# An adaLN block with linear attention: the state products taken head by head, in blocks of 32 columns

## The chip, the cores and the metric

The kernel runs on one core of one Trainium2 chip. Its metric is the device time of one execution in microseconds (us). A core has TensorE (PE in the profile; PEld is its weight load), VectorE (DVE), ScalarE (ACT), GpSimd (POOL) and SyncE (SP), each with a program of its own, and DMA queues that several of them issue to.

## The reference

x has 2048 rows of 640, in 32 heads of 20 columns.

```python
mod = (silu(c) @ w_mod).reshape(1, 6, 1, -1)          # sa, ca, ga, sb, cb, gb
h = layernorm(x) * (1 + ca) + sa
q, k, v = split_heads(h @ wqkv)                        # 32 heads of 20
phi_q = concat(softmax(q @ w_phi), softmax(-q @ w_phi))    # 40 features a head
phi_k = concat(softmax(k @ w_phi), softmax(-k @ w_phi))
kv  = einsum("bhsf,bhsd->bhfd", phi_k, v)              # the state, 40 x 20 a head
z   = einsum("bhsf->bhf", phi_k)
num = einsum("bhqf,bhfd->bhqd", phi_q, kv)
den = einsum("bhqf,bhf->bhq", phi_q, z) + 1e-6
x = x + ga * ((num / den) @ wo)
h = layernorm(x) * (1 + cb) + sb
x = x + gb * (relu(h @ w1 + b1) ** 2 @ w2 + b2)        # 1728 wide
```

## The kernel before

The 2048 rows are 16 row tiles of 128, worked in pairs (t and t + 1 for even t). The projections k, v and q (`proj`, its products on the line of `mm`, L80) are sums of three products of a high and a low part. Each tile's 640 columns are made in two halves, 384 and 256 (`CUT`); TensorE's pieces of it are pk, pv and pq.

For each tile, k and q become features: `spread` subtracts the maximum and the minimum of each head (eq and ek, 128 x 1280: for each sign 640 columns), `exps` takes exponentials on ScalarE, and for k `k_norm` (L448 to L450) divides on VectorE by the sums, the last step being one product of 1280 columns. ek of tile t is `EK[t]`.

*State products.* `v_out` (L426 to L429) copies v from PSUM to the tile `vt[t % 2]` on ScalarE, four copies a tile. `vt` has 11 units of 64 columns: the 20 columns of three heads, a column of ones, three of zeros (the last unit has two heads). `do_kv` then makes one float32 product for each unit (L457): its 64 columns of `vt` are the stationary side, the same three heads' 2 x 60 features in ek the moving one. The product also holds what one head's v makes with another head's features, which is not used; the column of ones makes z. Units with even numbers use the left 64 columns of TensorE, the odd ones the right 64, and the sums over all 16 tiles stay in two PSUM banks (kvp). `do_kv` runs for two tiles at once, eight times in all, behind the v projection of the next pair's first tile and ahead of its q projection. Each float32 product shows as two loads and two products in the profile.

*The switch.* After the last pair, three ScalarE copies bring the state to SBUF (kvs, L797 to L799). `make_z`, inside the q projection of tile 13, spreads the row of each z over 128 rows by products with a broadcast column of the identity, four products in two row tiles of TensorE (64 rows each, L823), and copies them to zb (L831 to L835). `kv_diags`, in the q projection of tile 14, turns kvs by five transposes of 128 columns (L844) and a small one (L845), and does a few turns for the modulation vectors (mc, L308). `kv_out` copies the turned tiles (kvt) to kvd on ScalarE, and `kv_mask5` and `kv_masks` multiply them on VectorE by masks that leave each head its own block.

*Numerators.* `e_prod` multiplies the features of q with zb (L884) and adds them up, `e_recip` inverts, `e_tail` (L909) and `e_main` scale the features; ut holds the last two heads' ones. TensorE turns them (`tail_turn` L936, `tr_e` L954), multiplies them with kvd (`tail_num`, `num`), and goes on with wo.

*What sets the order.* In the start, and again from the last pair's k projection on, every engine runs in the order in which the code is written. In tiles 2 to 13 TensorE runs in written order; the other engines' order comes from a scheduler that sets it by its own costs of the instructions. DMA goes over queues issued from SP, ACT and POOL.

Of the kernel before, what the change touches and what calls it, by code (L numbers as in the profile page):

```python
# [20 lines left out]
F = 1728  # L21
NT = S // P
# [31 lines left out]
def kernel(  # L54
# [37 lines left out]
    def heads(ap):  # L92
        return ap.rearrange("p (h d) -> p h d", d=DH)
# [25 lines left out]
    def row(tag, name):  # L119
        return (pc if tag in ("s3", "s4") else mem).tile([P, D], F32, tag=tag, name=name, bufs=BUFS[tag])  # L120
# [19 lines left out]
    def tp(name):  # L140
        return psA.tile([P, 512], F32, tag="tp", name=name)
# [38 lines left out]
    mask5 = pc.tile([80, 40], F32, name="mask5")  # L180
    pc.tile([P, 24], F32, name="gap3")
    for v in vt:
        nc.gpsimd.memset(v, 0.0)
        nc.gpsimd.memset(v[:, :, 60:61], 1.0)

    def head_mask(m, rows, n, at):

        m3 = m.rearrange("p (h d) -> p h d", d=DH)
        nc.gpsimd.affine_select(out=m3, in_=m3, compare_op=ALU.is_ge, fill=0.0, base=-at,
                                pattern=[[-DH, n], [0, DH]], channel_multiplier=1)  # L190
        nc.gpsimd.affine_select(out=m3, in_=m3, compare_op=ALU.is_ge, fill=0.0, base=DH - 1 + at,
                                pattern=[[DH, n], [0, DH]], channel_multiplier=-1)

    mtmp = row("s2", "mtmp")[:120, :60]
    nc.gpsimd.memset(mask, 0.0)
    nc.gpsimd.memset(mask[:, :60], 1.0)
    nc.gpsimd.memset(mtmp, 1.0)
    head_mask(mask[:, :60], 120, 3, 0)
    head_mask(mtmp, 120, 3, 60)
    nc.gpsimd.tensor_tensor(mask[:, :60], mask[:, :60], mtmp, op=ALU.add)  # L200
    nc.gpsimd.memset(mask5, 1.0)
    nc.gpsimd.memset(mtmp[:80, :40], 1.0)
    head_mask(mask5, 80, 2, 0)
    head_mask(mtmp[:80, :40], 80, 2, 40)
    nc.gpsimd.tensor_tensor(mask5, mask5, mtmp[:80, :40], op=ALU.add)


    nc.scalar.dma_start(bdc[:120, :120], bd)
    nc.scalar.dma_start(c_t, c)
# [92 lines left out]
    def mod_turn(part, p, *cs_):  # L302
        t = MT.setdefault(part, None) or row("s1", f"mt{part}")
        MT[part] = t
        a, n = cs_[0] * P, len(cs_) * P
        for i, c in enumerate(cs_):
            src = by_turn(MA[part])[:, c] if part in (3, 4) else MA[part][:, c * P : (c + 1) * P]
            nc.tensor.transpose(p[:, i * P : (i + 1) * P], src, ident)  # L308
        nc.scalar.activation(t[:, a : a + n], p[:, :n], AF.Copy)
# [79 lines left out]
    def t1(j, *ds, more=None):  # L389
        if 0 in ds:  # L390
            HT[j] = ht(f"hT{j}", j)
        p = tp(f"ta{j}_{ds[0]}")
        for k, d in enumerate(ds):
            t_in(XB[j], d, p[:, 256 * k : 256 * k + 256])
        if more:
            mod_turn(more[0], p[:, 256:], 4)
        for k, d in enumerate(ds):
            t_out(cols_a, HT[j], d, f"a{j}", p[:, 256 * k : 256 * k + 256])
        DONE[:] = newest(ET_.Activation), newest(ET_.DVE)
        if more:  # L400
            mod_sum(*more)

    def proj(nm, t, *between):
        p = pj(f"p{nm}{t}")
        j, i = divmod(t, 2)
        s = slice(i * P, (i + 1) * P)
        for h, (a, b) in enumerate(CUT):
# [12 lines left out]

    def do_v(t):
        v_out(t, proj("v", t))
# [28 lines left out]

    def do_kv(t):
        v, e = vt[t % 2], EK[t]
        for u, (o, n) in enumerate(UN):
            g, c = divmod(u, 2)
            a = 120 * (g % 4)
            nc.tensor.matmul(  # L457
                kvp[g // 4][64 * c : 64 * c + 64, a : a + 2 * n].rearrange("p (s n) -> p s n", s=2),
                v[:, u], e[:, :, o : o + n],
                start=(t == 0 and g % 4 == 0), stop=(t == NT - 1), skip_group_check=True,  # L460
            )

    def do_q(t, *between):
# [249 lines left out]
    for t in range(2, NT - 2):  # L713
# [13 lines left out]
        p = proj("v", t, *([(1, 0, lambda: t1(j + 1, 4))] if t == NT - 3 else []))  # L727
        if i == 0:
            do_kv(t - 2)
            do_kv(t - 1)  # L730
# [73 lines left out]
    def bank(nm):  # L804
        return psB.tile([P, 512], F32, tag="m", name=nm)
# [6 lines left out]
    nc.gpsimd.memset(kv_t[96:, :640], 0.0)  # L812
    nc.gpsimd.tensor_copy(
        kv_t[96:, :640].rearrange("p (b n) -> p b n", n=64)[:, :, 60:],
        ident[96:, None, 120:124].to_broadcast([32, 10, 4]),
    )
    def make_z():
        at = [(c, b) for b in range(2) for c in range(2)]
        ps = {}
        for c, b in at:  # L820
            r, a, n = slice(64 * c, 64 * c + 64), 480 * b, ((480, 200), (480, 120))[c][b]
            p = ps[c, b] = tp("z") if len(ps) == 3 else bank(f"z{c}_{b}")
            nc.tensor.matmul(p[:, :n], ident[r, 64 * c + 60 : 64 * c + 61].to_broadcast([64, P]),  # L823
                             kvs[r, a : a + n], start=True, stop=True)
        for c, b in at:
            g0, m, p = 4 * b, (4, 1)[b], ps[c, b]
            for h in range(2):
                dst = zb[:, h, 120 * g0 : 120 * (g0 + m)].rearrange("p (g c n) -> p g c n", c=2, n=60)[:, :, c]
                src = p[:, : 120 * m].rearrange("p (g s n) -> p g s n", s=2, n=60)[:, :, h]
                if h:  # L830
                    nc.vector.tensor_copy(dst, src)  # L831
                else:
                    nc.scalar.activation(dst, src, AF.Copy)
            if (c, b) == (0, 1):
                nc.vector.tensor_copy(zb[:, :, 600:640], p[:, 120:200].rearrange("p (s n) -> p s n", s=2))  # L835

    q_out(q0 + 1, proj("q", q0 + 1, (0, 9, make_z)))

    kvt = [None, None]

    def kv_diags():
        kvt[:] = [bank(f"kvt{b}") for b in range(2)]
        for g in range(5):
            nc.tensor.transpose(kvt[g // 4][:120, (g % 4) * P : (g % 4) * P + P], kvs[:, 120 * g : 120 * g + 120], ident)  # L844
        nc.tensor.transpose(kvt[1][:80, P : P + 40], kvs[:40, 600:680], ident[:40, :40])  # L845
        mod_turn(5, kvt[1][:, 2 * P :], 4)
        mod_turn(5, bank("mc5"), 0, 1, 2, 3)

    def kv_out():
        nc.scalar.activation(kv5, kvt[1][:80, P : P + 40], AF.Copy)  # L850
        for b, (g0, g1) in enumerate(((0, 4), (4, 5))):
            nc.scalar.activation(kv_t[:120, P * g0 : P * g1], kvt[b][:120, : (g1 - g0) * P], AF.Copy)

    def kv_mask5():
        nc.vector.tensor_tensor(kv5, kv5, mask5, op=ALU.mult)

    def kv_masks():
        k = kv_t[:120, : 5 * P].rearrange("p (g n) -> p g n", n=64)
        nc.vector.tensor_tensor(k, k, mask[:, None, :].to_broadcast([120, 10, 64]), op=ALU.mult)


    ET, EU, EPT, OT = {}, {}, {}, {}
# [332 lines left out]
    e_recip(1)  # L1195
    load_e(3)
    do_q(q0 + 2, (1, 0, kv_diags))
    kv_out()
    e_tail(1)
    kv_mask5()  # L1200
    e_main(1)
# [599 lines left out]
```

## Time and profile before

| | |
|---|---|
| three runs | 751.80, 751.52, 750.88 us; median 751.52 |
| the profiled execution | 751.83 us, of which the span is 750.1 |
| TensorE's granted clock | 1.000 |
| busy: TensorE, VectorE, ScalarE, GpSimd | 744.9, 601.4, 457.5, 169.0 us |
| share of the span | 99%, 80%, 61%, 23% |

The span runs from the first to the last instruction that the profile records; the execution's time has a little around it. A row of the groups reads: line, engine, operation, output <- input by the program's names, TensorE's tile (rows*columns), shape and type, count | busy us, mean ns of one | idle us ahead of them. A row of the chain reads: start, length, engine, what, line, and how many instructions in a row. A row of the windows reads: window and its length, then for PE, PEld, DVE, ACT, POOL the busy us and the count, and behind them TensorE's clock, the DMA share and GB/s. Busy times of TensorE's products overlap where blocks of it run side by side, so the mean of one is then no cost of one.

### The profile page before, as it was taken

To read this page: it belongs to the slowest core of one execution; us is meant where nothing else is said; L and a number is where in the kernel's file an instruction comes from. 1 tells how busy PE (TensorE), PEld (TensorE's weight loads), DVE (VectorE), ACT (ScalarE), POOL (GpSimd) and SP (SyncE) were. 2 spreads that over 40 slices of the span, in tenths; PEclk is the share of its full clock that TensorE was granted. 3 is DMA by queue.
4 is the path that set the end of the run, shared out by engine and by line. 5 is a ranking of instruction groups with operands and counts; after the bars stand their busy time and mean duration, and the time that the engine had idled before them with its cause. 6 is when DMAs were issued, how large, how long until landed. Compare 5 with 4: busy or idle time off the path is not lost.

```text
span 750.1 us, 15320 instructions
## 1 busy us (share of the span) xinstructions
PE 744.9 (99%) x5854; PEld 728.3 (97%) x5854; DVE 601.4 (80%) x1089; ACT 457.5 (61%) x1065; POOL 169.0 (23%) x355
## 2 busy tenths in 40 slices
PE   9999999999999999999999999999999999999998
PEld 9999999999999998998999999999999999999997
DVE  6598987988998899999665778777777776777766
ACT  5767666667863355557587766475574756647431
POOL 3000101000100237647303040132221313223110
PEclk9999999999999999999999999999999999999999
DMA  9811432343432254663885576797667767667461
GB/s 330 335 36 77 155 93 81 107 140 107 137 101 81 57 189 160 150 148 109 195 236 183 158 212 227 252 343 204 180 198 200 222 183 227 191 172 218 127 184 36
DMA packets 58796, 126.39 MB, mean 168 GB/s; under 512 B 7438, under 2 KB 16403, under 8 KB 58723
## 3 DMA queue, kind: packets, MB, share of 16 engines
q1 hardware_dynamic: 38636, 79.20, 32.2%
q0 software_dynamic: 17504, 40.90, 21.8%
q10 hardware_dynamic: 2583, 5.30, 1.9%
q8 instruction: 46, 0.75, 0.4%
q14 instruction: 27, 0.22, 0.1%
HBM read 100.74 MB, written 29.89 MB: 174 GB/s over the span
## 4 chain that ended last, share of the span: by engine, by line
PE 98%; ACT 1%; DVE 1%; POOL 0%; issue 0%; ACTq 0%; POOLq 0%
PE up L80 25%; PE acc L80 18%; PE pq L80 9%; PE pk L80 9%; PE pv L80 9%; PE pwo L80 9%; PE acc3x L80 5%; PE kvp L457 3%; PE te L954 2%; PE numa L80 1%; PE foldk L282 1%; PE numb L80 1%; PE ta L364 1%; PE foldq L282 1%; PE warm L625 1%; PE mrow L586 1%
## 5 line engine op out<-in xcount | busy, mean ns | idle before, releaser
L80 PE MATMUL up<-h,w 128*128 128x256 f32 x1640 | 204.6, 276 | 0.1
L80 PEld LDWEIGHTS up<-h,w 128*128 128x128 f32 x1640 | 196.5, 188 | 0.7 <-DVE h L90 0.5
L1350 ACT ACTIVATE ft<-up,b_t 128x256 f32<-128x256 f32 x104 | 49.0, 471 | 96.0 <-PE up L80 95.6
L80 PE MATMUL acc<-w,ra 128*128 128x384 f32 x452 | 97.5, 335 | 0.0
L80 PE MATMUL pwo<-wo,ot 128*128 128x384 f32 (+1 forms) x480 | 78.4, 314 | 0.0
L1351 DVE TENSOR_TENSOR ft<-ft 128x256 f32<-128x256 f32 x104 | 43.8, 421 | 43.1 <-ACT ft L1350 41.4
L80 PE MATMUL pq<-wq,hT 128*128 128x384 f32 (+1 forms) x480 | 75.6, 312 | 0.0
L80 PEld LDWEIGHTS acc<-w,ra 128*128 128x128 f32 x452 | 72.7, 188 | 0.8 <-DVE ra L90 0.6
L80 PE MATMUL pk<-wk,hT 128*128 128x384 f32 (+1 forms) x480 | 72.7, 308 | 0.0
L80 PEld LDWEIGHTS pwo<-wo,ot 128*128 128x128 f32 x480 | 69.7, 188 | 2.8 <-issue 2.7
L80 PEld LDWEIGHTS pq<-wq,hT 128*128 128x128 f32 x480 | 71.1, 188 | 0.6 <-issue 0.2
L80 PE MATMUL pv<-wv,hT 128*128 128x384 f32 (+1 forms) x480 | 71.6, 306 | 0.0
L80 PEld LDWEIGHTS pk<-wk,hT 128*128 128x128 f32 x480 | 70.5, 188 | 0.4 <-issue 0.2
L80 PEld LDWEIGHTS pv<-wv,hT 128*128 128x128 f32 x480 | 70.0, 188 | 0.0
L90 DVE TENSOR_TENSOR ra<-ft,ra 128x384 fp32r<-128x384 f32 (+2 forms) x86 | 36.8, 449 | 32.6 <-ACT ra L1374 20.0
L1460 POOL DMA_DIRECT2D ring_a<-td_a x34 | 18.5, 543 | 116.9 <-PE acc L80 103.6
L1374 ACT ACTIVATE ra<-ft 128x384 fp32r<-128x384 f32 x48 | 25.2, 526 | 28.4 <-DVE ft L1351 22.4
L80 PE MATMUL acc3x<-w,ra 128*128 128x256 f32 x231 | 39.5, 278 | 0.0
L80 PEld LDWEIGHTS acc3x<-w,ra 128*128 128x128 f32 x231 | 37.2, 188 | 0.0
L1365 DVE TENSOR_TENSOR ft<-ft 128x128 f32<-128x128 f32 x136 | 33.3, 286 | 1.2
L448 DVE TENSOR_REDUCE sk<-ek 128x64 f32<-128x1280 f32 x16 | 23.7, 1484 | 12.8 <-ACT ek L443 10.8
L341 POOL TENSOR_SCALAR sma<-sma 128x2 f32<-128x2 f32 x6 | 1.8, 298 | 137.2 <-ACT xb L340 137.2
(270 smaller groups left out, 1470.2 us busy)
## 6 DMA issues: line engine op xcount, KB each, us to landing
ring_c<-td_c POOLq DMA_DIRECT2D x34, 384.0 KB, 3.8
ring_a<-td_a POOLq DMA_DIRECT2D x34, 384.0 KB, 3.4
ring_b<-td_b POOLq DMA_DIRECT2D x34, 256.0 KB, 3.6
esp<-eq SPq DMA_DIRECT2D x12, 640.0 KB
el<-esp SPq DMA_DIRECT2D x12, 640.0 KB
rw<-in_w SPq DMA_DIRECT2D x23, 320.0 KB
wm<-in_w_mod SPq DMA_DIRECT2D x20, 320.0 KB
xb<-in_x SPq DMA_DIRECT2D x8, 640.0 KB
```

Of the source, the lines that this page charges most:

```text
L80: nc.tensor.matmul(o, a, b, start=first and i == 0, stop=last and i == len(terms) - 1, skip_group_check=skip,)
L90: (eng or nc.vector).tensor_tensor(out_lo, full, hi.bitcast(F32), op=ALU.subtract)
L282: nc.tensor.matmul(p[g // 3][:, (g % 3) * 120 : (g % 3) * 120 + n], r, bd_t[:120, g * 120 : g * 120 + n], start=True, stop=True,)
L364: nc.tensor.transpose(p[:, i * P : (i + 1) * P], src, ident)
L448: nc.vector.tensor_reduce(s, heads(flat(e)), axis=AX.X, op=ALU.add)
L457: nc.tensor.matmul(kvp[g // 4][64 * c : 64 * c + 64, a : a + 2 * n].rearrange("p (s n) -> p s n", s=2), v[:, u], e[:, :, o : o + n], start ...
L954: nc.tensor.transpose(p[:124, a : a + P], EU[2 * j + i][:, 2 * g + c, :124], ident)
L1350: nc.scalar.activation(r, p, AF.Relu, bias=b1_t[:, f : f + 1])
L1351: nc.vector.tensor_tensor(r, r, r, op=ALU.mult)
L1365: nc.vector.tensor_tensor(t[:, o], t[:, a], t[:, b], op=op)
L1374: nc.scalar.activation(a[:, 0, :3], t[:, :3], AF.Copy)
L1460: nc.gpsimd.dma_start(RING[j, n, r], TD[n][r].bitcast(F32R))
```

## The change

The state products are made head by head. `vt` holds 21 columns a head, its 20 columns of v and a one. Head h goes to the 32-column block (h // 3) % 4 of TensorE: 21 stationary columns, and as the moving side its own 2 x 20 features. `HEAD_AT` orders the heads so that four neighbours in the program go to four blocks. All sums lie in one PSUM bank, 360 columns wide at most. The v projection is cut at 380 and 260 columns in place of 384 and 256, so that heads stay whole, and the weights' columns keep their natural order. `v_out` has two copies a tile for four, and kvs one for three.

z comes from four row tiles of 32 rows, of 360, 360, 320 and 240 columns. `kv_diags` has three transposes for six, all in one bank; `kv_out` is gone, and the masks' products (`kv_own`) read the turned state in PSUM and write kvd.

```diff
-UN = [(60 * u, 60) for u in range(10)] + [(600, 40)]
-NU = len(UN)
+NU = 11
+HEAD_AT = [(h % 3 + 3 * (h // 12), h // 3 % 4, h) for h in range(H)]
+HEAD_AT.sort()
 CUT = ((0, 384), (384, D))
-VCOLS = [*range(360), *range(600, 624), *range(360, 600), *range(624, D)]
+V_CUT = ((0, 380), (380, D))
...
-    vt = [pc.tile([P, NU, 64], F32, name=f"vt{i}") for i in range(2)]
+    vt = [pc.tile([P, NU * 64], F32, name=f"vt{i}")[:, : H * (DH + 1)].rearrange("p (h d) -> p h d", d=DH + 1) for i in range(2)]
...
     def v_out(t, p):
         v = vt[t % 2]
-        nc.scalar.activation(v[:, 0:6, :60], p[0][:, :360].rearrange("p (g d) -> p g d", d=60), AF.Copy)
-        nc.scalar.activation(v[:, 6:10, :60], p[1][:, :240].rearrange("p (g d) -> p g d", d=60), AF.Copy)
-        nc.scalar.activation(v[:, 10, :24], p[0][:, 360:384], AF.Copy)
-        nc.scalar.activation(v[:, 10, 24:40], p[1][:, 240:256], AF.Copy)
+        for h, (a, b) in enumerate(V_CUT):
+            nc.scalar.activation(v[:, a // DH : b // DH, :DH], heads(p[h][:, : b - a]), AF.Copy)
...
     def do_kv(t):
         v, e = vt[t % 2], EK[t]
-        for u, (o, n) in enumerate(UN):
-            g, c = divmod(u, 2)
-            a = 120 * (g % 4)
+        for g, c, h in HEAD_AT:
+            m = min(3, H - h // 3 * 3) * DH
+            a = 120 * (g // 3) + g % 3 * DH
             nc.tensor.matmul(
-                kvp[g // 4][64 * c : 64 * c + 64, a : a + 2 * n].rearrange("p (s n) -> p s n", s=2),
-                v[:, u], e[:, :, o : o + n],
-                start=(t == 0 and g % 4 == 0), stop=(t == NT - 1), skip_group_check=True,
+                kvp[0][32 * c : 32 * c + DH + 1, a - g % 3 * DH : a - g % 3 * DH + 2 * m].rearrange("p (s n) -> p s n", s=2)[:, :, h % 3 * DH : h % 3 * DH + DH],
+                v[:, h], e[:, :, DH * h : DH * (h + 1)],
+                start=(t == 0 and g == 0), stop=(t == NT - 1), skip_group_check=True,
             )
...
-    nc.scalar.activation(kvs[:, :480], kvp[0][:, :480], AF.Copy)
-    nc.scalar.activation(kvs[:, 480:600], kvp[1][:, :120], AF.Copy)
-    nc.scalar.activation(kvs[:64, 600:680], kvp[1][:64, 120:200], AF.Copy)
+    nc.scalar.activation(kvs[:, :360], kvp[0][:, :360], AF.Copy)
...
     def make_z():
...
-            nc.tensor.matmul(p[:, :n], ident[r, 64 * c + 60 : 64 * c + 61].to_broadcast([64, P]),
-                             kvs[r, a : a + n], start=True, stop=True)
+        for c in range(4):
+            r, n = slice(32 * c, 32 * c + DH + 1), (360, 360, 320, 240)[c]
+            p = tp("z") if c == 3 else bank(f"z{c}")
+            nc.tensor.matmul(p[:, :n], ident[r, 32 * c + DH : 32 * c + DH + 1].to_broadcast([DH + 1, P]),
+                             kvs[r, :n], start=True, stop=True)
...
     def kv_diags():
-        kvt[:] = [bank(f"kvt{b}") for b in range(2)]
-        for g in range(5):
-            nc.tensor.transpose(kvt[g // 4][:120, (g % 4) * P : (g % 4) * P + P], kvs[:, 120 * g : 120 * g + 120], ident)
-        nc.tensor.transpose(kvt[1][:80, P : P + 40], kvs[:40, 600:680], ident[:40, :40])
+        kvt.append(bank("kvt"))
+        for q in range(3):
+            nc.tensor.transpose(kvt[0][:120, q * P : q * P + P], kvs[:, 120 * q : 120 * q + 120], ident)
...
-    def kv_out():
-        nc.scalar.activation(kv5, kvt[1][:80, P : P + 40], AF.Copy)
-        for b, (g0, g1) in enumerate(((0, 4), (4, 5))):
-            nc.scalar.activation(kv_t[:120, P * g0 : P * g1], kvt[b][:120, : (g1 - g0) * P], AF.Copy)
+    def kv_own(out, n, m):
+        rows = m.shape[0]
+        k = kvt[0][:rows, : 12 * 32].rearrange("p (u r) -> p u r", r=32)[:, n, None, :DH]
+        shape = [rows, n.stop - n.start, m.shape[1], DH]
+        nc.vector.tensor_tensor(out, k.to_broadcast(shape), m[:, None, :, None].to_broadcast(shape), op=ALU.mult)
```

The order of instructions shows three places. The first is TensorE at the second pair: pv is the v projection of tile 4, kvp the state products of tiles 2 and 3 (ek is the features, vt the values), pq the q projection. Before:

```order
L80 MATMUL pv_1_1199<-wv_583,hT_975 128x256 x3
L457 MATMUL kvp_76<-ek_916,vt_104 64x120 x8
L457 MATMUL kvp_77<-ek_916,vt_104 64x120 x2
L457 MATMUL kvp_77<-ek_916,vt_104 64x80
L457 MATMUL kvp_76<-ek_1069,vt_105 64x120 x8
L457 MATMUL kvp_77<-ek_1069,vt_105 64x120 x2
L457 MATMUL kvp_77<-ek_1069,vt_105 64x80
L80 MATMUL pq_0_1277<-wq_317,hT_975 128x384 x3
```

And now:

```order
L81 MATMUL pv_1_1230<-wv_578,hT_1008 128x260 x3
L81 MATMUL pv_1_1230<-wv_580,hT_1008 128x260 x3
L448 MATMUL kvp_76<-ek_949,vt_104 21x2x20 x32
L448 MATMUL kvp_76<-ek_1100,vt_105 21x2x20 x32
L81 MATMUL pq_0_1348<-wq_314,hT_1008 128x384 x3
L81 MATMUL pq_0_1348<-wq_325,hT_1008 128x384 x3
```

The place is the same; a tile has 32 products of 2 x 20 columns where it had 10 of 120 and one of 80.

The second is TensorE where tile 14's q projection holds the turns of the state; kvt is the turned state, and mc and the products with wm belong to the modulation vectors. Before:

```order
L844 MATMUL kvt_3208<-ident,kvs 120x128 x4
L844 MATMUL kvt_3209<-ident,kvs 120x128
L845 MATMUL kvt_3209<-ident,kvs 80x40
L308 MATMUL kvt_3209<-ident,wm_4_2821 128x128
L308 MATMUL mc_3219<-ident,wm_4_2821 128x128 x4
```

And now:

```order
L81 MATMUL pq_0_3490<-wq_408,hT_2790 128x384 x3
L833 MATMUL kvt<-ident,kvs 120x128 x3
L301 MATMUL kvt<-ident,wm_4_3042 128x128
L301 MATMUL mc_3514<-ident,wm_4_3042 128x128 x4
L81 MATMUL pq_1_3491<-wq_314,hT_2790 128x256 x3
```

Two of the five transposes and the small one are gone.

The third is VectorE, where the scheduler's order changes though no instruction of the stretch does: tile 11's k features (ek with the sums sk), with tile 11's q (eq, mxq), tile 12's k maxima (mxk) and the weights of wo (rwo). Before:

```order
L448 TENSOR_REDUCE sk_2511<-ek_2490 128x64
L90 TENSOR_TENSOR hT_2383<-hfa_4_2540,hT_2383 128x256
L313 TENSOR_REDUCE cols_b<-mt_2307 128x5
L449 RECIPROCAL sk_2511<-sk_2511 128x64
L437 TENSOR_REDUCE mxq_2563<-q_2557 128x32
L438 TENSOR_REDUCE mxq_2563<-q_2557 128x32
L547 TENSOR_SCALAR cols_b<-cols_b 128x5
L501 TENSOR_TENSOR rwo_2705<-rwo_2705,ga_b 128x640
L450 TENSOR_TENSOR ek_2490<-ek_2490,sk_2511 128x1280
```

And now:

```order
L439 TENSOR_REDUCE sk_2694<-ek_2673 128x64
L91 TENSOR_TENSOR hT_2568<-hfa_4_2723,hT_2568 128x256
L306 TENSOR_REDUCE cols_b<-mt_2494 128x5
L428 TENSOR_REDUCE mxq_2746<-q_2740 128x32
L429 TENSOR_REDUCE mxq_2746<-q_2740 128x32
L440 RECIPROCAL sk_2694<-sk_2694 128x64
L538 TENSOR_SCALAR cols_b<-cols_b 128x5
L492 TENSOR_TENSOR rwo_2928<-rwo_2928,ga_b 128x640
L431 TENSOR_TENSOR eq_2745<-q_2740,mxq_2746 128x640 x2
L428 TENSOR_REDUCE mxk_2916<-k_2755 128x32
L429 TENSOR_REDUCE mxk_2916<-k_2755 128x32
L441 TENSOR_TENSOR ek_2673<-ek_2673,sk_2694 128x1280
```

The last multiplication of tile 11's ek stands four instructions later, behind tile 11's eq and tile 12's maxima.

More of the change, by code (lines that the diff above doesn't have):

```diff
@@ L175, with head_mask @@
     bb = const.tile([P, D], F32, name="bb")
-    vt = [pc.tile([P, NU, 64], F32, name=f"vt{i}") for i in range(2)]
+    vt = [pc.tile([P, NU * 64], F32, name=f"vt{i}")[:, : H * (DH + 1)].rearrange("p (h d) -> p h d", d=DH + 1) for i in range(2)]
     rs_q = pc.tile([P, NT, 2 * H], F32, name="rs_q")
     mask = pc.tile([120, 64], F32, name="mask")
-    mask5 = pc.tile([80, 40], F32, name="mask5")
+    mask5 = pc.tile([80, 40], F32, name="mask5")[:, :2]
     pc.tile([P, 24], F32, name="gap3")
     for v in vt:
[L183 to L205, printed above, removed]
+        nc.gpsimd.memset(v[:, :, DH :], 1.0)
+    def head_mask(m, n, at):
+        nc.gpsimd.memset(m, 1.0)
+        nc.gpsimd.affine_select(out=m, in_=m, compare_op=ALU.is_ge, fill=0.0, base=-at,
+                                pattern=[[-DH, n]], channel_multiplier=1)
+        nc.gpsimd.affine_select(out=m, in_=m, compare_op=ALU.is_ge, fill=0.0, base=DH - 1 + at,
+                                pattern=[[DH, n]], channel_multiplier=-1)
+    mtmp = row("s2", "mtmp")
+    mask = mask[:, :3]
+    for m, t, n in ((mask, mtmp[:120, :3], 3), (mask5, mtmp[:80, :2], 2)):
+        head_mask(m, n, 0)
+        head_mask(t, n, DH * n)
+        nc.gpsimd.tensor_tensor(m, m, t, op=ALU.add)
     nc.scalar.dma_start(bdc[:120, :120], bd)
@@ L401, in t1, with proj @@
             mod_sum(*more)
-    def proj(nm, t, *between):
+    def proj(nm, t, *between, cut=CUT):
         p = pj(f"p{nm}{t}")
@@ L406, in proj @@
         s = slice(i * P, (i + 1) * P)
-        for h, (a, b) in enumerate(CUT):
+        for h, (a, b) in enumerate(cut):
             terms = []
@@ L726 @@
                 next(parts)
-        p = proj("v", t, *([(1, 0, lambda: t1(j + 1, 4))] if t == NT - 3 else []))
+        p = proj("v", t, *([(1, 0, lambda: t1(j + 1, 4))] if t == NT - 3 else []), cut=V_CUT)
         if i == 0:
@@ L817, in make_z @@
     def make_z():
[L818 to L823, printed above, removed]
-                             kvs[r, a : a + n], start=True, stop=True)
[L825 to L830, printed above, removed]
+        ps = []
+        for c in range(4):
[3 more added lines that the diff above has]
+                             kvs[r, :n], start=True, stop=True)
+            ps.append(p)
+        for c, p in enumerate(ps):
+            m = 3 if c < 2 else 2
+            for i in range(2):
+                dst = zb[:, i, :600].rearrange("p (u n) -> p u n", n=60)[:, c : c + 4 * m - 3 : 4]
+                src = p[:, : 120 * m].rearrange("p (q s n) -> p q s n", s=2, n=60)[:, :, i]
+                if i:
                     nc.vector.tensor_copy(dst, src)
@@ L1197 @@
     do_q(q0 + 2, (1, 0, kv_diags))
-    kv_out()
     e_tail(1)
```

20 lines of the change are left out of this document (10 added, 10 removed).

## The prediction

> **What bounds the kernel now.** I read the page's busy times and its chain first, then the chain in order of time, then the groups with their shapes kept apart, and last the stretches on which the change works.
>
> ```profile
> PE 744.9 (99%) x5854; PEld 728.3 (97%) x5854; DVE 601.4 (80%) x1089; ACT 457.5 (61%) x1065; POOL 169.0 (23%) x355
> PE 98%; ACT 1%; DVE 1%; POOL 0%; issue 0%; ACTq 0%; POOLq 0%
> ```
>
> TensorE is busy 744.9 of 750.1 us, and 98% of the chain that ended last is TensorE's own work. So a microsecond taken from TensorE's stream is a microsecond of the end, as long as nobody is late for it. The profiled execution took 751.83 us (span 750.1 and 1.73 around it), 0.31 above the 751.52 median; my sum is made against 751.83.
>
> **What the state products cost.** The chain in order of time has eight pieces of them, one for each pair of row tiles, all alike; these are the first and the last, and behind them the pieces of the switch to the numerators that the change also touches.
>
> ```profile
> 60.92 2.47 PE kvp L457 x43
> ...
> 248.34 2.47 PE kvp L457 x43
> 252.59 1.34 PE z L823 x7
> 259.61 0.55 PE kvt L844 x5
> 260.16 0.16 PE kvt L845
> 260.58 0.44 PE mc L308 x4
> ```
>
> The last row gives a price: four 128-column transposes take 0.44 us, 0.11 each, 0.86 ns a moving column. The next rows give the shapes of the state products.
>
> ```profile
> L457 PE MATMUL kvp<-ek,vt 128*64 128x120 f32 x320 | 19.2, 270 | 0.0
> L457 PE MATMUL kvp<-ek,vt 128*64 128x80 f32 x32 | 4.8, 233 | 0.0
> L457 PEld LDWEIGHTS kvp<-ek,vt 128*64 128x64 f32 x352 | 19.0, 137 | 1.0
> L586 PEld LDWEIGHTS mrow<-wm,cs 128*32 128x32 f32 x100 | 3.0, 109 | 0.5 <-PE kvp L364 0.2 <-PE pk L80 0.2
> ```
>
> 352 records stand for 16 tiles of 11 products: each float32 product makes two passes. Per tile the left block of 64 columns has 5 x 120 + 80 = 680 moving columns, the right 600. For two tiles and two passes that is 2720 and 2400 columns. At 0.86 ns one after the other they would take 4.40 us; the row says 2.47. The blocks run side by side, and the longer sets the time: 2720 x 0.86 = 2.34 us, which leaves 0.13 for entry and exit.
>
> Do four blocks also run side by side? The profile of before has products in blocks of 32 columns, the mrow ones of the start.
>
> ```profile
> 17.86 0.85 PE L586 MATMUL mrow<-wm,cs 128*32 128x128 f32 x20
> 18.64 1.31 PE L364 MATMUL kvp<-ident,xb 128*128 128x128 f32 x10
> ```
>
> Ten full-width passes of 128 columns take 1.31 us, yet twenty in blocks of 32 columns take 0.85. One after the other they would need 2.2. Their longest block has 6 of the 20 passes: 6 x 0.11 plus the tail of the last. Four blocks do run at once.
>
> **The change, step by step.**
>
> State products. A head is 21 stationary columns (20 of v and a one) against 2 x 20 = 40 moving ones, in block (h // 3) % 4. Per tile the blocks have 9, 9, 8 and 6 heads. The longest makes 9 x 2 passes x 2 tiles = 36 passes of 40 columns, 1440 columns in place of 2720: 1440 x 0.86 = 1.24 us, 1.37 with the 0.13 of entry and exit. For 36 passes in place of 24 I allow 0.06 (an estimate of 5 ns for each more): 1.43. Saved: 2.47 - 1.43 = 1.04 a pair, 8.3 us in eight. Bounds: 1.37 if a pass has no fixed part (8.8 us in all); from above the weight loads. A load of 64 columns takes 137 ns and one of 32 columns 109, so 28 ns for 32 columns, 18 for 21. Beside the 34 ns of the block's pass ahead it fits; none hidden would add 36 x 0.018 = 0.65, 2.08 a pair, and leave 3.1 us of the gain. I take the hidden one, as in the mrow rows, whose loads of 32 columns cost nothing visible.
>
> Handing out. The new pair is 128 passes and 128 loads where 44 and 44 were. What the trace says of the rate is a row of the sequencer:
>
> ```profile
> L457 PE MATMUL kvp<-ek,vt x352: 232/266/318, 60.8 to 250.6; 128*64 128x120 f32 x152, 128*64 128x80 f32 x24
> L457 PEldq EVENT_SEMAPHORE  x4: 51/51/51, 60.9 to 248.3; - x4
> ```
>
> This wait stands ahead of the second tile, behind 22 loads and 22 passes, and the sequencer is at it by 60.9, 0.1 us after the first pass at 60.8. At that rate 256 instructions take some 0.6 us, below the 1.24 that their columns need.
>
> z by four row tiles. Before, each row tile streamed 480 + 200 columns at most, twice: 1360 x 0.86 = 1.17 of the 1.34 us. Now the longest has 360: 720 x 0.86 = 0.62, 0.79 with the same 0.17 around it. Saved 0.55; nothing, if only two row tiles run at once (1360 columns again), since the trace shows two and not four. I take 0.55, by the column blocks.
>
> Transposes. Three of five remain and the small one goes: 2/5 of 0.55 and 0.16, saved 0.38.
>
> Costed at nothing: v's cut at 380/260, still 640 columns a tile (bounds: the two halves of a pv piece, no gain or loss beyond 0.1). ScalarE loses two short copies of 0.19 us a tile and three copies of the kvt tile; kvs becomes one copy. ScalarE isn't on the chain; kvs is covered by the nine pq products ahead of z. The mask products read PSUM on VectorE, 600 elements for 640. POOL's masks get smaller; POOL is 23% busy. Lost cover would cost the 0.19 us copies themselves.
>
> **Who is late next.** VectorE, at two places.
>
> ```profile
> 90.66:120.47 29.81, 29.81 (x235) 29.59 (x234) 26.18 (x34) 18.94 (x43) 2.79 (x4) 1.00 0.32 103
> 181.17:212.00 30.83, 30.83 (x244) 30.62 (x243) 28.88 (x40) 25.67 (x58) 5.02 (x7) 1.00 0.39 126
> 206.61 1.49 DVE L450 TENSOR_TENSOR ek<-ek,sk 128x1280 f32<-128x1280 f32 x1
> 208.01 1.56 DVE L440 TENSOR_TENSOR eq<-q,mxq 128x640 f32<-128x640 f32 x2
> 209.48 0.81 DVE L437 TENSOR_REDUCE mxk<-k 128x32 f32<-128x640 f32 x1
> ```
>
> A pair's period is 29.8 us with VectorE busy 26.2 of them (third busy column), and 28.9 of 30.8 in the fullest. With 1.04 less these are 91% and 97%. In that fullest pair the new order puts tile 11's last multiplication by 1/sum (L450) behind the eq pair and the next tile's two reductions, 1.5 + 1.5 us later. Before, it ended at 208.1 and TensorE asked for it at 212.0. Of 3.9 us some 0.9 are left, and 0.6 more while the even tile's products run ahead of it. For stalls in this part I allow 0.4 us.
>
> ```profile
> 254.03 0.85 DVE L831 COPY zb<-z 128x240 f32<-128x240 f32 x3 [0.59 <-ACT zb L833]
> 255.19 1.49 DVE L884 TENSOR_TENSOR scr<-el,zb 128x1280 f32<-128x1280 f32 x1
> 264.07 0.24 DVE L909 TENSOR_TENSOR ut<-el,dn 128x80 f32<-128x80 f32 x1
> 265.16 0.38 PE L936 MATMUL tail<-ident,ut 128*80 128x128 f32 x2
> 275.42 0.24 DVE L909 TENSOR_TENSOR ut<-el,dn 128x80 f32<-128x80 f32 x1
> 276.19 0.38 PE L936 MATMUL tail<-ident,ut 128*80 128x128 f32 x2
> ```
>
> From z on VectorE works without a break up to the first tails. It moves forward with the end of z, TensorE by the transposes' 0.38 more. The slack was 265.16 - 264.31 = 0.85 at the first tail and 276.19 - 275.66 = 0.53 at the second, so 0.47 and 0.15 would remain. ScalarE copies that stand between are as tight, so I allow 0.4 here.
>
> Sum: 8.3 + 0.55 + 0.38 = 9.2, less 0.8 of new waits: 8.4. 751.83 - 8.4 = **743.4 us**.
>
> **Rivals.**
>
> Slower: the passes can't be handed out fast enough. The place is each pair's 128 passes; the point from which it decides is (2.47 - 0.13) / 128 = 18 ns a pass. The densest long stretch that before shows is the mrow one, with starts over 0.85 - 0.27 us (277 ns is one pass, the row below), 30 ns each. At 30 ns a pair costs 3.97 us, 1.50 more, 12.0 in eight; less 0.9 from z and the transposes, 763 us. Against it: those 30 ns are what their columns need, and the sequencer's row above.
>
> ```profile
> L586 PE MATMUL mrow<-wm,cs 128*32 128x128 f32 x100 | 4.0, 277 | 0.0
> ```
>
> [...]
>
> Loads not hidden: 3.1 in place of 8.3, with the rest 4.0, few new waits: 748 us. Against it, the mrow rows.
>
> VectorE takes over from the fullest pair on: the last three pairs' 3.1 us are lost, and the 0.8 stays: 746.5 us. For it speaks the 97%; against, that 1.9 us of its idle time in that pair are left even now.
>
> Only two blocks at once, so that the split does nothing: 64 heads in two rows of blocks, 2560 columns, 2.33 us a pair, 1.1 saved; with 0.55 and 0.38, 749.8 us. Against it, the twenty passes in 0.85 us.
>
> **How the numbers follow.** Forecast 0.70; VectorE 0.12; loads 0.08; slower 0.06; two blocks 0.04. The predicted time is the forecast's. Its own range is 742.1 (no new waits, passes without a fixed part: 9.7 saved) to 744.7 (waits of 1.6 us and nothing from z: 7.1 saved). The whole range must hold 8 in 10 and takes in VectorE's case and the loads': 741.9 to 748.3. A measurement here can tell about 0.2% (1.5 us) from no change. The first three cases are faster by more, 0.90, and I give 0.01 of it back; two blocks, at 1.7 us, is split between faster and same, and with errors of size same has 0.04; slower 0.06 and 0.01 for what I haven't seen: 0.07.
>
> **What would show it.** Right: eight pieces of state products of 1.4 us with 127 or so passes each; z at 0.8; three kvt transposes; no new idle of TensorE over 0.5 us at the second tile of a pair and at the tails; VectorE over 90% busy in the pairs. Wrong: pieces of 2.1 (loads) or of 2.3 (two blocks) or above 2.5 us (handing out); pieces of 1.4 with TensorE idle behind them, waiting for ek or ut (VectorE).

## The result, and the profile after

The changed kernel takes 747.11 us (median of 4 runs, 746.64 to 747.72) against 751.20 for the kernel before on the same chip: a ratio of 0.9942, 95% interval 0.993 to 0.9955. That is 4.1 us less, inside my range, but half of the 8.4 that I forecast and outside the likeliest case's own range (742.1 to 744.7). The profiled execution took 746.64 us with a span of 744.9, 5.2 less than before's 750.1.

The chain in order of time (start, length, what) has the first piece of state products where it was expected:

```profile
56.37 4.40 PE pv L81 x30
60.77 1.41 PE kvp L448 x125
62.17 0.90 PE pq L81 x4
```

The page's busy times:

```profile
PE 738.1 (99%) x6523; PEld 720.6 (97%) x6523; DVE 598.8 (80%) x1089; ACT 453.1 (61%) x1028; POOL 169.1 (23%) x352
```

TensorE is still 99% busy. But the page's chain that ended last is no longer TensorE's alone, 88% in place of 98:

```profile
PE 88%; DVE 6%; ACT 3%; POOL 1%; issue 1%; ACTq 0%; DVEq 0%; POOLq 0%
```

In order of time it leaves TensorE for two long stretches, from 85 to 125 us, up to where transposes (ta) wait for ScalarE, and from 245 to 271 us, up to the second tail, and for shorter ones later. The piece of state products has gone from 2.47 to 1.41 us, against 1.43 forecast. Six of the eight are like this one. But the piece of v ahead of it (30 products) says 4.40; the same row in before's chain:

```profile
56.62 4.30 PE pv L80 x30
```

One of the eight pieces is not like the others. This is the timeline of TensorE at tiles 6 and 7; the bracket gives the idle time ahead of a row and what ended it.

```profile
147.84 0.76 PE L81 MATMUL pv<-wv,hT 128*128 128x260 f32 x5
148.53 1.19 PE L448 MATMUL kvp<-ek,vt 128*21 128x40 f32 x91
149.91 0.48 PE L448 MATMUL kvp<-ek,vt 128*21 128x40 f32 x9 [0.19 <-issue]
150.76 0.29 PE L448 MATMUL kvp<-ek,vt 128*21 128x40 f32 x6 [0.38 <-issue]
151.38 0.59 PE L448 MATMUL kvp<-ek,vt 128*21 128x40 f32 x22 [0.33 <-issue]
```

It stops after 91 of its 128 passes, then goes on in bits: 3.38 us from the first pass to the next product, 1.97 more than its neighbours. The profile shows no semaphore that is waited for ("issue"). z and the transposes of the state, in the timeline after (before, the prediction's lines have 1.34 us of z, and 0.55 and 0.16 of kvt):

```profile
247.92 0.87 PE L811 MATMUL z<-kvs,ident 21*128 21x360 f32 x8
254.17 0.49 PE L833 MATMUL kvt<-ident,kvs 128*120 128x128 f32 x3
```

And the first tail now waits:

```profile
259.43 0.27 PE L925 MATMUL tail<-ident,ut 128*80 128x128 f32 x1
259.96 0.31 PE L925 MATMUL tail<-ident,ut 128*80 128x128 f32 x1 [0.26 <-DVE ut L898]
```

Adding up, for each name on TensorE, the times from each product's start to the next one's, in both traces, gives where the 5.2 us of the profiled executions came from (us):

| term | forecast | measured |
|---|---|---|
| state products, eight pieces | -8.3 | -8.53, if all were 1.405 |
| the fourth piece, held up | 0 | +1.97 |
| the eighth, second tile late by its vt | 0 | +0.11 |
| z | -0.55 | -0.53 |
| transposes of the state and what stands with them | -0.38 | -0.53 |
| pv (cut at 380 and 260) | 0 | +1.40 |
| first and second tail | +0.4 | +0.74 |
| waits for ek in the pairs | +0.4 | 0 |
| one q piece ending late (the transposes behind it, ta, wait for ScalarE) | 0 | +0.28 |
| start (foldk, ahead of all that was changed) | 0 | -0.52 |
| all else | 0 | +0.4 |

### The profile page after: what moved, and what is told of

Same layout as the page of the kernel before. It is cut to its first block, busy times and chain, and to the rows that moved or that the text cites. A ratio compares the mean times of both kernels' runs of the same rounds, so it can differ in the third digit from the quotient of the medians.

```text
span 744.9 us, 16612 instructions
## 1 busy us (share of the span) xinstructions
PE 738.1 (99%) x6523; PEld 720.6 (97%) x6523; DVE 598.8 (80%) x1089; ACT 453.1 (61%) x1028; POOL 169.1 (23%) x352
## 4 chain that ended last, share of the span: by engine, by line
PE 88%; DVE 6%; ACT 3%; POOL 1%; issue 1%; ACTq 0%; DVEq 0%; POOLq 0%
PE up L81 25%; PE acc L81 18%; PE pk L81 8%; PE pwo L81 8%; PE pv L81 8%; PE pq L81 6%; PE acc3x L81 5%; PE te L943 2%; PE kvp L448 1%; DVE dn L875 1%; PE foldk L275 1%; PE numa L81 1%; PE ta L357 1%; DVE scr L873 1%; PE foldq L275 1%
## 5 line engine op out<-in xcount | busy, mean ns | idle before, releaser
L81 PE MATMUL pv<-wv,hT 128*128 128x380 f32 (+1 forms) x480 | 73.0, 309 | 0.0
```

The lines of the kernel that those rows point to most:

```text
L81: nc.tensor.matmul(o, a, b, start=first and i == 0, stop=last and i == len(terms) - 1, skip_group_check=skip,)
```

## The experiments

The theory after the result was: the large terms came as forecast, and two that I had at zero took back 3.4 us, the cut of v and a piece held up beside a fetch of instructions. All kernels start from the changed one except where it is said. Each ratio is to the kernel before on the same chip; medians of different kernels come partly from different chips.

### Cut v at another place

```diff
-V_CUT = ((0, 380), (380, D))
+V_CUT = ((0, 400), (400, D))
```

> The changed kernel with v cut at 400 and 240 columns in place of 380 and 260. In the changed kernel a pv piece takes 4.40 us against 4.30 before; the products of 260 columns start 120 ns apart where those of 256 were 114, and those of 380 take the same 173 as 384. Theory A (columns are paid in steps, 16 of them or a 64-byte boundary; 400 and 240 are both whole): pieces of 4.30 again, 16 tiles x 0.10 = 1.6 us less than the changed kernel, about 745.5. Rival B (a product of over 256 columns pays one more start, of one up to 256 it does not): also 4.30, since only one half is over 256. Rival C (the tiles of v cost what they do for another reason, such as the output's layout): pieces stay at 4.40, 747.1. Rival D (a product narrower than 256 columns runs slower): 240 columns cost more than 114 ns, pieces over 4.40, slower than the changed kernel.

746.13 us (745.11 to 747.53; 0.9922 of before, 0.9904 to 0.9941). But the pieces of v did not get shorter; from the chain of this run:

```profile
56.55 4.41 PE pv L81 x30
```

The starts are 183 ns apart at 400 columns and 112 at 240: 295 for the pair, like 173 + 120 at 380 and 260, and more than the 287 of 384 and 256. Theories A and B fall, and D too, for 240 columns cost no more than 256 (114). C's number is right, but its reason (the layout of v's output) isn't shown. Why the median is 1.0 us below the changed kernel's isn't shown: in the profiled execution (746.93 us) the fourth piece of state products was held up for 0.30 us in place of 1.97, but in the second half a product waited 1.2 us for a ring of weights, and its span is 0.3 us longer than the changed kernel's.

### Cut k at many places

```diff
+K_AT = [384, 384, 380, 382, 368, 400, 320, 352, 376, 388, 384, 372, 384, 396, 384, 384]
+K_CUT = [((0, n), (n, D)) for n in K_AT]
...
-        to_sb(proj("k", t), PK[t])
+        to_sb(proj("k", t, cut=K_CUT[t]), PK[t], K_CUT[t])
```

> The changed kernel with the k projection of each row tile cut at another column: 384, 384, 380, 382, 368, 400, 320, 352, 376, 388, 384, 372, 384, 396, 384, 384 for tiles 0 to 15 (the rest of the 640 in the second half); read from the starts of the products in the trace. Known: 256 columns 114 ns, 384 columns 173, 260 columns 120, 380 columns 173. Theory A (steps of 16 columns, about 7.2 ns a step): 372, 376, 380 and 382 cost what 384 does, 388 and 396 what 400 does (180); 258, 260, 264 and 268 what 272 does (120); 244 and 252 what 256 does (114); 320/320 costs 144 each, and 352/288 sums to 287 like 384/256. Theory B (one more start of 6 ns once a product is over 256 columns, else 0.417 ns a column): 320/320 costs 147 each, 294 in all; 352/288 sums to 293; 258 costs 120, and 376 costs 3 less than 384. Theory C (the second half starts off a 64-byte boundary): 368/272 and 400/240 and 352/288 and 320/320 are cheap, all others pay 6 ns in the second half only.

The medians from start to start, in ns, with the sum of a pair (one run, 749.55 us):

| first + second half | ns | sum |
|---|---|---|
| 384 + 256, four tiles | 173 to 174 + 113 to 118 | 286 to 292 |
| 380 + 260 | 173 + 120 | 293 |
| 382 + 258 | 178 + 120 | 298 |
| 376 + 264 | 173 + 122 | 295 |
| 372 + 268 | 171 + 122 | 293 |
| 368 + 272 | 169 + 127 | 296 |
| 352 + 288 | 162 + 132 | 294 |
| 320 + 320 | 147 + 147 | 294 |
| 388 + 252 | 178 + 116 | 294 |
| 396 + 244 | 179 + 113 | 292 |
| 400 + 240 | 184 + 112 | 296 |

None of the three theories holds: 320 + 320 should have been cheap by A and C, and 376 by B, 3 ns under 384. (B's 0.417 ns a column is an estimate: 384 columns at 173 ns and 256 at 113 to 114, less its 6 ns, leave 0.41 to 0.42.) The same width differs by up to 5 ns with its place in the program (256 columns: 113 in some tiles, 118 in others), so one tile a width can't rank the cuts closely; no cut is below what 384 + 256 takes. Why 384 + 256 is cheap stays open. The firm numbers are those of v, over 16 tiles each: 4.30 us a piece at 384 + 256, 4.40 at 380 + 260, 4.41 at 400 + 240.

### Keep 384 and 256

```diff
-V_CUT = ((0, 380), (380, D))
+V_CUT = CUT
...
-        for h, (a, b) in enumerate(V_CUT):
-            nc.scalar.activation(v[:, a // DH : b // DH, :DH], heads(p[h][:, : b - a]), AF.Copy)
+        nc.scalar.activation(v[:, 0:19, :DH], heads(p[0][:, :380]), AF.Copy)
+        nc.scalar.activation(v[:, 20:, :DH], heads(p[1][:, 16:256]), AF.Copy)
+        nc.scalar.activation(v[:, 19, :4], p[0][:, 380:384], AF.Copy)
+        nc.scalar.activation(v[:, 19, 4:DH], p[1][:, :16], AF.Copy)
```

> The changed kernel with v cut at 384 and 256 columns as before, head 19 copied from both halves (four ScalarE copies for two). The cut at 400 and 240 did not bring the 0.10 us a tile back: 183 + 112 ns against 173 + 120 at 380 and 260. Theory A (384 and 256 are the cheap pair, 173 + 114): pv pieces of 4.30 in place of 4.40, 1.6 us less in TensorE's sum over 16 tiles. The time follows if the copies stay covered: 745.5, give or take 0.8, since the piece held up by the instruction fetch has varied from 1.7 to 4.2 us between kernels. Rival (two more copies of 0.2 us a tile come too late for the state products of the pair's second tile, or ScalarE's other work is late): pv pieces of 4.30, but new waits for vt, ek or hT of over 1 us together.

```profile
56.34 4.30 PE pv L81 x30
```

The pieces are 4.30 again and pv's sum falls by 1.24 us, as theory A had it (1.6 expected). Yet the median is 749.1 (746.49 to 749.24; 0.9958, 0.9943 to 0.9973), 2 us above the changed kernel's, though the two intervals overlap. The rival's waits stay under its 1 us: 0.17 us for ek at the sixth piece, and the products ta wait once for ScalarE, 0.4 us. What made the profiled execution slow is the fourth piece, held up more than ever, and what followed it. The windows have, behind the engines, TensorE's granted clock:

```profile
147.00:150.00 3.00, 2.31 (x93) 2.00 (x92) 3.00 (x4) 2.38 (x7) 0.91 (x3) 1.00 0.08 5
150.00:153.00 3.00, 1.81 (x49) 1.36 (x49) 1.03 (x3) 0.94 (x3) 0.18 (x1) 0.95 0.00 0
153.00:156.00 3.00, 3.00 (x12) 3.00 (x11) 0.73 (x2) 2.86 (x5) 0.00 (x0) 0.50 0.91 300
156.00:159.00 3.00, 3.00 (x23) 3.00 (x23) 1.93 (x2) 0.49 (x1) 0.00 (x0) 0.98 0.77 247
```

TensorE is busy 2.31 and 1.81 of 3 us, and then the clock is 0.50 for some 3.4 us (the third window, and what the 0.95 and 0.98 beside it make): products of 384 columns start 320 ns apart in place of 173. The piece took 4.41 us, 3.00 over its neighbours, and the slow clock added 1.6 behind it. In the changed kernel's own trace TensorE is busy 2.81 and 2.29 of 3 us in the same two windows, with 1.97 us lost at the same place, and the clock stays at 1.00 there and in the two windows behind. What sets the half clock off isn't shown.

### The instruction fetch, and the small writes ahead of it

The page of the changed kernel has this row of a queue of instructions (packets, MB, share of 16 engines):

```profile
q8 instruction: 51, 0.84, 0.5%
```

That is 16 KB a packet. TensorE has 13046 loads and products, so a packet holds some 256 of its instructions (an estimate from these two numbers, if the queue serves TensorE alone; before's page has 46 packets for 11708, 255 a packet). A pair's state products are 256 instructions now, 128 loads and 128 passes, within 1.4 us. Fetches take about 1 us (the median is 1.04), but the one at this place took 3.42. This is the DMA view of 147 to 153 us, whose last column is the share of 16 engines: 3.6% of 16 x 6 us is 3.4 us.

```profile
q8 instruction: 1, 0.02, 3.6%
```

And the queue on SyncE shows what else was under way, the gate vector's way to DRAM and back:

```profile
141.93 0.38 SPq L324 DMA_DIRECT2D gate<-gate_a  x1
151.46 0.34 SPq L325 DMA_DIRECT2D ga_b<-gate  x1
```

The write has 640 packets of 4 bytes. They are sent by 143.3, but the read that waits for their end is issued at 151.46. The trace has the fetch from 149.51 to 152.92. The experiment turns the gate vector on TensorE and writes 5 rows:

```diff
+    def turned_row():
+        p = tp("gate_t")[:NC, :P]
+        nc.tensor.transpose(p, gate_a, ident)
+        nc.scalar.activation(gate_r, p, AF.Copy)
+        nc.sync.dma_start(GD[0], gate_r)
+        nc.sync.dma_start(ga_b, GD[0].rearrange("c p -> (c p)")[None, :].to_broadcast([P, D]))
...
-        7: lambda: (spread_row(0, gate_a, ga_b), mod_mac(4, 3)),
-        8: lambda: mod_mac(4, 4),
+        7: lambda: mod_mac(4, 3),
+        8: lambda: (turned_row(), mod_mac(4, 4)),
```

> The changed kernel with the gate vector turned by one product on TensorE and written to DRAM in 5 rows, one tile later, in place of 640 packets of 4 bytes. In the changed kernel the state products of tiles 6 and 7 took 3.38 us where the others take 1.41, with TensorE idle inside although ek and vt were there; a fetch of 16 KB of instructions, which took 3.42 us where others take about 1, lay beside it, and the writes of 4 bytes were not yet done. Theory A (the burst of 256 instructions runs the engine dry, and the fetch is held up behind the small writes): that piece falls to 1.4 to 1.8 us, the fetch to about 1 us; with one product of about 0.15 us added the time is 1.5 to 1.9 below the changed kernel, about 745.4. Rival B (the fetch is slow at this place of the program or this time whatever the writes do): the piece stays at 3.4, time 747.2. Rival C (the wait is for ek, vt or VectorE): stays as well, with TensorE's wait named.

The fourth piece falls from 3.38 to 1.406 us, and the fetch to 0.97. The time doesn't follow: 747.17 (746.94 to 747.32; 0.9938, 0.9923 to 0.9953). The edit had a fault of its own, 1.35 us at ta, which the timeline shows; another 0.4 us went in the start, ahead of the edit.

```profile
155.28 0.60 PE L357 MATMUL ta<-ident,xb 128*128 128x128 f32 x4
156.99 0.27 PE L529 MATMUL gate_t<-ident,gate_a 128*5 128x128 f32 x1 [1.11 <-ACT hfa L368]
```

The new product shares the one bank of ta and waits for ScalarE to empty it. With `p = kvp[2][:NC, :P]`, a bank of the state that is free by then:

> The turned gate vector again, its product now into a PSUM bank that is free, so that it waits for no other tile (in the run before it waited 1.1 us for the bank of the tile ta). Theory A (the long piece of state products is the instruction fetch held up behind the 640 writes of 4 bytes): all eight pieces 1.4 to 1.6 us, none at 3.4, no new wait over 0.4 us ahead of tile 10, and 1.6 to 2.0 us less than the changed kernel: 745.1 to 745.5. Rival (VectorE and ScalarE take back what TensorE gains, as in tile 9's pair): the piece is short, but waits of TensorE for ek, hT or ta within the next two pairs add up to over 1 us; time 746.5 or more.

745.92 us (744.91 to 748.56; 0.9931, 0.991 to 0.9951), 0.4 above the range of theory A. The profiled execution's timeline at the place:

```profile
147.81 0.76 PE L81 MATMUL pv<-wv,hT 128*128 128x260 f32 x5
148.51 1.48 PE L448 MATMUL kvp<-ek,vt 128*21 128x40 f32 x128
149.91 0.73 PE L301 MATMUL mc<-ident,wm 128*128 128x128 f32 x4
```

One row in place of four, no idle time. In that trace TensorE stands 1.99 us ahead of the changed kernel's at the switch; 0.22 goes at the first tail, and 0.6 much later, where a product of the second half waits for a ring of weights. The runs spread more than the gain. So the pieces show that the hold-up goes with the small writes; its price in the median, 1.2 us, is known only roughly.

What TensorE waits for while it stands idle isn't shown. In all five kernels whose fourth piece is held up (the changed one and the runs with 400, with the widths, with 384, and with VectorE's order) the idle time begins 0.1 to 0.2 us after this fetch does, so the two belong together. But the burst doesn't need what the fetch brings: in the run with the free bank all 128 passes are done at 149.9, before the same fetch (the twelfth of its queue in both traces) begins at 151.88; and in the changed kernel the last pass starts at 151.8, 1.1 us before the fetch lands. Nor do the small writes make it land later: it lands 4.4 us behind the piece's first pass with them and 4.3 without. With them it begins earlier and is under way for longer.

The control is the same edit in the kernel before:

> The kernel before with the gate vector turned by one product into the free bank and written in 5 rows, and nothing else. Theory A (the 640 small writes only cost where the engine runs dry, which the state products of before, 88 instructions a pair in 2.47 us, never do, though a fetch took 3.41 us there too): the fourth piece is 2.47 us with them and without, the fetch falls to about 1 us, and the time stays, 751.5, or 0.2 more for the added product. Rival (the writes cost by themselves, through TensorE's or the queues' other transfers): 750 or less.

0.9998 of before (0.9989 to 1.0007; 10 runs). The DMA view of 150 to 156 us, of before and of this run:

```profile
q8 instruction: 1, 0.02, 3.5%
```

```profile
q8 instruction: 1, 0.02, 1.0%
```

The fetch was as slow before the change (3.41 us), and it cost nothing: the piece, 88 instructions, takes 2.47 us with the small writes and without. Here neither cost the piece anything by itself, the small writes at 2.47 us or the burst at 1.406; together they held up the fourth piece by 0.30 to 3.00 us in five kernels.

### The heads in another order

```diff
-HEAD_AT.sort()
+HEAD_AT.sort(key=lambda x: (x[1], x[0]))
```

> The changed kernel with the heads in another order: all heads of the first block of 32 columns, then all of the second, and so on, in place of four neighbours for four blocks. Same products, same columns. Theory A (a block's passes run one after the other, and instructions are handed out in order with little room to run ahead): a tile's blocks come one after the other, 32 heads x 2 passes x 2 tiles x 35 ns = 4.5 us a pair in place of 1.41; a bit less with room to run ahead. 8 x 3.1 = 25 us more, about 772. Theory B (each block has a queue that holds all of a tile's passes): 1.4 to 1.6 us a pair, no change of the time.

763.54 us (one run), some 16 more than the changed kernel where 25 were expected. The timeline at tiles 6 and 7:

```profile
154.78 0.76 PE L81 MATMUL pv<-wv,hT 128*128 128x260 f32 x5
155.47 3.89 PE L448 MATMUL kvp<-ek,vt 128*21 128x40 f32 x128
159.30 0.73 PE L301 MATMUL mc<-ident,wm 128*128 128x128 f32 x4
```

All eight pieces take 3.82 us from the first pass to the next product. These are the changed kernel's own passes, and they are slower than before's 2.47. Theory A, though under its 4.5: 30 ns a pass in place of 35, and whether blocks overlap at their ends isn't shown. So the gain needs both: four blocks, and neighbours in the program in different blocks. And the fourth piece is no longer than the others, though its fetch took 2.67 us, nearly all of it beside the piece: at a third of the pace nothing is held up.

### VectorE ahead of z

```diff
-    q_sums(q0)
-    gb_mac(2)
+    gb_mac(2)
+    q_sums(q0)
```

In the changed kernel, this is VectorE from the sums (rs_q) to the copies of z:

```profile
246.52 1.49 DVE L476 TENSOR_REDUCE rs_q<-eq 128x64 f32<-128x1280 f32 x1 [0.70 <-ACT eq L435]
247.92 1.79 DVE L291 SCALAR_TENSOR_TENSOR wm<-wm,cs,wm 128x640 f32<-128x640 f32 x2
249.64 0.78 DVE L820 COPY zb<-z 128x180 f32<-128x180 f32 x3
```

z is there at 248.72, but VectorE still has its two products for the modulation vector.

> The changed kernel with VectorE's last two products for the modulation vector (wm, 0.9 us each) ahead of the sums of tile 12's q features in place of behind them. In the changed kernel VectorE stands idle for 0.70 us ahead of these sums, then makes the two products, and begins to copy z to zb at 249.64, 0.92 us after z is there (248.72); TensorE then waits 0.46 us for ut at the first tail and 0.28 at the second. Theory A (VectorE is late for z by what stands ahead of it, and the tails wait for that): zb begins about 0.55 us earlier, the tails' waits fall from 0.74 to 0.1 to 0.3 us, and the time by 0.5. Rival B (the tails wait for GpSimd's products between VectorE's, not for z): waits stay at 0.7.

The first tail's time falls from 0.59 to 0.14 us, 0.45 of the 0.74; the second tail's doesn't change. Theory A for the first, not for the second. The median is 747.47 (746.92 to 748.01; 0.9942, 0.9927 to 0.9957): nothing gained, and in the profiled execution the fourth piece took 4.16 us, 0.78 more than in the changed kernel's, which is more than the 0.45.

### The cut in the kernel before

```diff
 CUT = ((0, 384), (384, D))
+V_CUT = ((0, 380), (380, D))
...
-        v_out(t, proj("v", t))
+        v_out(t, proj("v", t, cut=V_CUT))
```

> The kernel before with v cut at 380 and 260 columns and nothing else (its units of three heads stay, the last unit is copied as 20 and 20 columns). Theory A (the cut costs 0.10 us a tile by itself): pv pieces of 4.40 in place of 4.30, 16 x 0.10 = 1.6 us more, 753.1. Rival (it costs only beside the changed layout of vt or the changed copies): pieces of 4.30, 751.5.

753.01 us against 752.27, 0.7 more by the medians and 1.1 by the ratio: 1.0014 (1.0005 to 1.0024; 10 runs). That is less than the 1.6 expected. pv's sum in the trace grows by 1.39 us, the same as in the changed kernel (1.40), and the pieces are 4.40:

```profile
56.34 4.40 PE pv L81 x30
```

So the pieces cost by the cut itself, whatever the layout of vt: theory A. That settles rival C of the first experiment too.

### All three together

> The changed kernel with all three: the gate vector turned into the free bank and written in 5 rows, v cut at 384 and 256 with four copies, VectorE's two products for the modulation vector ahead of the sums. If the three terms add up: 1.97 (piece held up by the fetch) + 1.6 (pv) + 0.45 (first tail) - 0.15 (the product added) = 3.9 below the changed kernel, 743.2, which is the time I had predicted for the change itself. Rival (the engine runs into the next limit: VectorE in the pairs, or the rings of weights in the second half, which made TensorE wait 1.2 us in the run with the 400 and 240 cut): 744.5 to 746, with such waits named in the trace.

744.69 us (744.00 to 744.92): 0.9906 of before, 0.989 to 0.9923. This beats both kernels, by 7.1 us and by some 2.4. Of the 3.9 expected, 2.4 came, and the time lies in the rival's range. The trace has the fourth piece at 1.41, pv at 4.30 and the first tail at 0.14, as expected; against that stand, beside the changed kernel's trace, 0.2 us at one q piece where ta waits for ScalarE, 0.55 at the q piece behind the fourth piece, 0.17 at the sixth piece, where the second tile's ek comes late, 0.26 at a k piece, 0.46 in the start, ahead of all edits, and small waits later. So its "next limit" is there, but spread over several small ones. ScalarE with its two more copies a tile is one; the 0.55 has one idle stretch with nothing to issue:

```profile
150.57 3.48 PE pq L81 x22
154.06 0.20 issue
154.25 1.21 PE pq L81 x8
```

## Why the prediction was right, and where it was wrong

**State products: right, and the price too.** Pieces of 1.405 us against 1.43. The passes have starts 10 ns apart over the engine (128 in 1.27 us), 35 ns in the longest block (36 of them). So the rival in which they can't be handed out falls: 10 ns is under the 18 from which it decides, and it comes from the longest block's 35. The 5 ns for each pass more in the forecast were my estimate, and no run shows them; the pieces lie 0.035 us above the 1.37 without them. Loads were hidden: the rival of 2.08 us a pair falls. "Only two blocks at once", at 2.33, falls as well.

**Handing out: right for the pace, wrong in what I looked at.** The step "at that rate 256 instructions take some 0.6 us, below the 1.24 that their columns need" held in its outcome: seven of eight pairs have their 256 instructions in 1.4 to 1.5 us. Its 0.6 was no measurement, since the row doesn't show when the sequencer began with the 44; and the row was from a pair of 88 and could not tell what a burst of 256 meets. In the fourth pair it meets the long fetch behind the small writes and stands idle. This is the term that I hadn't: 1.97 us in the profiled execution, and from 0.30 to 3.00 in the other kernels that keep the small writes and the burst. With 5 rows it is gone; what TensorE waits for there stays open.

**"v's cut at 380/260, still 640 columns a tile": the step that failed.** It was costed at nothing, with "no gain or loss beyond 0.1". A piece did change by just that, 0.10, and I didn't multiply it by the 16 pieces: 1.6 us by the pieces, 1.4 in the sums. A bound on a piece is no bound on the kernel.

**z and the transposes: right on TensorE** (0.53 for 0.55; 0.53 for 0.38), so four row tiles do run at once. But of z's 0.53 VectorE passed nothing on at first, since it was busy when z came. That made the first tail's wait 0.46 where I had some 0.2, and the second's 0.28. I had summed 0.4 here: 0.74.

**VectorE in the pairs: the right place, and just not late.** No wait for ek shows in the changed kernel's trace, so the 0.4 wasn't needed, and the rival in which VectorE takes over falls. But the margin that I put at 0.9 us and more was nearly gone: in the sixth pair the second tile's ek ended 5.06 us ahead of its first pass before, and 0.13 us now. In the runs with 384 and with all three that piece waited 0.17 us for it. Of "costed at nothing", the copies to vt lost their cover in one place: the eighth piece waits 0.11 us for the second tile's.

Together: 8.4 forecast; plus 0.2 from the products, 0.15 from the transposes and 0.4 for ek; less 1.97, 1.40, 0.34 at the tails and 0.39 at the eighth piece and ta; that is 5.1. The start's 0.5 in its favour, which has nothing to do with the change, and 0.4 of small things against it make the 5.2 of the profiled execution. The median run has 4.1. That it lies in my range is in part luck: the range reached up to 748.3 for VectorE's case and the loads', and neither came. What used that room, the held-up piece and the cut, was no term of mine.

## What to carry to other kernels

The small products ran four abreast in blocks of 32 columns when neighbours in the program went to different blocks: 1.41 us a pair, against 3.82 with neighbours in one block. The longest block set the time, 36 passes at 35 ns. A burst of 256 short instructions had a price that no group's row shows, 1.97 us in one pair: where TensorE stands idle with "issue", look at the queue of instructions, at whether a fetch is under way beside the burst, and at the small writes ahead of it. And an edit "of the same number of columns" is to be counted in its own rows, times the number of pieces, before it is put down at zero.

## What the runs showed of the hardware that I had not expected

Behind a write of 640 packets of 4 bytes, all sent within 1.4 us, a fetch of 16 KB of instructions was under way for 2.3 to 3.8 us in eight kernels, where it took 0.95 to 0.97 in the four without; in the changed kernel and the run with the free bank it landed equally late (elsewhere in these traces single fetches took up to 2.6 us). Cutting 640 columns at 384 costs 0.10 us less for 30 products than at 380 or 400, and the widths alone don't explain it. A stall of 3.0 us in bits, with TensorE busy for 2.31 and 1.81 us of its two windows of 3, was followed by some 3.4 us of half the clock in one kernel; one of 2.75 us in another wasn't (its granted clock is 1.00).
